# A two-stage spectral kernel: one row tile per PSUM bank in the second stage, and reloadable weight buffers filled first

## The chip, the cores and the metric

The kernel runs on one core of one Trainium2 chip. The metric is the device time of one execution in microseconds (us), the median of several runs. A ratio is the mean time of one kernel's fast runs over the mean time of the other kernel's fast runs of the same rounds, so it is not quite the ratio of the medians quoted beside it. A run counts as slow when it lies more than 1.5% above the fastest run of its kernel; the ratios leave slow runs out, the medians quoted do not.

## The reference

```
x: (8, 3264, 192)                     8 batches, 3264 positions, 192 channels
a  = causal 7-tap convolution of x, softmaxed taps per head (8 heads of 24 channels)
X  = rfft(a, axis=1)[:, :64]          64 modes
Y  = X @ (w_r + i w_i)[mode]          a 192x192 complex matrix for each mode
y  = irfft(Y, n=3264)
u  = a + y
out = u + relu(u @ w_ch)
```

The kernel never forms `u`. It keeps `a` in bf16 and uses `u @ w_ch = a @ w_ch + y @ w_ch`, with the 64 modes multiplied by `w_ch` beforehand ("weight products").

## The kernel before

It has three stages.

1. *First stage* (to 80 us): x is loaded by GpSimd's DMA queue, convolved by banded matmuls, and projected on 64 cosines and 64 sines.
2. *Mix stage* (80 to 111 us): sixteen groups of four modes. Each group needs 2 x 288 KB of weights. "Mix g" is 12 short matmuls. In between PE transposes `a` into `cc` (channels on the partitions) and the cosine and sine table, in "jobs" of one PSUM bank each; VectorE and ACT copy the banks out.
3. *Second stage* (from 111 us): 50 "duos" of two row blocks x two batches, one item for the row ends ("h"), and two items that compute further weight products. For each duo PE adds a channel part `a @ w_ch` and a table part (`g`, the modes already multiplied by `w_ch`), ACT applies relu, PE adds the table part `y`, VectorE adds `a` and writes an output buffer that SyncE stores.

The matmuls of the second stage contract over 64 partitions, so two of them are issued as a pair of row tiles, on partitions 0 to 63 and 64 to 127. In the profile before the two of a pair run side by side: pairs of 192 columns follow one another every 0.08 us and pairs of 384 columns every 0.16 us, and single matmuls of 384 columns over 128 partitions also every 0.16 us. Before the change an item's bank holds both batches of one block, and its sums need both halves of the partitions: channels 0 to 63 and cosines below, channels 64 to 127 and sines above. The kernel lets the two row tiles work on two banks and then swap, and at each swap PE waits ("turn"; in the profile before a weight load stands still for 0.29 us there). Here no two row tiles of the second stage work on one bank at the same time, so what that would do is not shown. The turns in the kernel:

```python
def both(duo, zt, first, which, begin=False, end=False):
    lists = (z_pieces(duo[first], 0, which), z_pieces(duo[1 - first], 1, which))
    old = held.get(id(zt))
    if old is not None and old[0] != first and not begin:
        turn(old[1])                  # PE waits for its own last matmuls on these banks
    for k in range(...):
        for row in range(2):
            ...
            nc.tensor.matmul(zt[:, first ^ row, cols], l, r, ...)
```

The weights of the mix stage have nine buffers. Four lie in the part of `cc` that is filled last ("late") and can be used once; five lie in an arena and are used again:

```python
wts = [... for a, n in ((late, NL), (arena, NW)) for i in range(n)]     # NL = 4, NW = 5
def wbuf(g): return wts[g] if g < NL else wts[NL + (g - NL) % NW]
def mix(g):
    ...                                # 12 matmuls
    if g >= NL:
        load_w(g + NW)                 # group 9 is issued after mix 4
```

Of the kernel before, what the change touches and what calls it, by code (L numbers as in the profile page):

```python
# [19 lines left out]
def kernel(  # L20
# [32 lines left out]
    def sb(name, shape, dtype, **kw):  # L53
# [5 lines left out]
    NW = 5  # L59
# [3 lines left out]
    CB = 2 * NF + 1 + NT  # L63
    cc = sb("cc", [NQ, CB, P], BF16)
    cm, ct = cc[:, :, 0:CB - NT, :], cc[:, :, CB - NT:CB, :]
    ftab = sb("ftab", [NT + 1, 2 * MODES], BF16)

# [4 lines left out]
    zw = mixa[:, 0:2 * B * D].rearrange("p (b t d) -> p b t d", b=B, t=2)  # L72
# [3 lines left out]
    wt2 = sb("wt2", [D], BF16)  # L76
# [5 lines left out]
    ymix = [sb(f"ymix{i}", [2, D], BF16) for i in range(2)]  # L82
# [3 lines left out]
           for a, n in ((late, NL), (arena, NW)) for i in range(n)]  # L86

    def wbuf(g):
        return wts[g] if g < NL else wts[NL + (g - NL) % NW]

    NO = 7
    OB = 2 * 2 * 2 * D
    outs = [arena[:, OB * i:OB * (i + 1)].bitcast(F32).rearrange("p (k d) -> p k d", k=2) for i in range(NO)]
    pos = [0]
# [23 lines left out]
    midx = temp(MODES, F32)  # L118

# [37 lines left out]
    hs = [xall[HALF:P, NT:NSLOT:NT, 0, :], xall[0:HALF, NT:NSLOT:NT, 1, :]]  # L157
# [12 lines left out]
    for a in hs:  # L170
        nc.vector.memset(a, 0.0)
# [47 lines left out]
    for i in range(2):  # L219
        src = bass.AP(tensor=x.tensor, offset=x.offset + (i * S + P * NF) * D,  # L220
                      ap=[[D, HALF], [2 * S * D, NQ], [1, D]])
        nc.gpsimd.dma_start(out=xall[HALF * i:HALF * i + HALF, NT:NSLOT:NT, i, :], in_=src)
# [11 lines left out]
    for q in range(NQ):  # L234
        nc.gpsimd.memset(ct[0:HALF, q, NF, HALF:P], 0.0)
        nc.gpsimd.memset(ct[HALF:P, q, NF, 0:HALF], 0.0)
# [4 lines left out]
    for i in range(2):  # L241
        nc.gpsimd.dma_start(out=wt2[64 * i:64 * i + 64, :], in_=moe_w_ch[P:D, :])
# [12 lines left out]
    def conv_step(q, t0, n, half, step):  # L255
# [8 lines left out]
        for j in range(2):  # L264
            for own in (True, False):
# [6 lines left out]
                if own:  # L272
                    ms = [(LO, LO, o, cur, 0), (UP, UP, o, cur, 0)]
                    if last:
                        ms.append((UP, UP, o[:, n - 1, 1, :], xall[:, s0 + n - 1, 1, dsl], 64))
                else:
                    ms = [(LO, UP, o, cur, 0), (UP, LO, o[:, k0:n, :, :], prev, 64)]
# [29 lines left out]
    def dft_unit(q, t0, n):  # L307
        xp = low[0][:, 0:2 * D]
        for t in range(t0, t0 + n):
            if t < NF:  # L310
                nc.tensor.matmul(xp, ftab[:, t, :], xall[:, slot(q, t), :, :], start=(t == 0), stop=False,  # L311
                                 skip_group_check=True)
            else:
                for i in range(2):
                    nc.tensor.matmul(xp[:, D * i:D * i + D], ftab[:, NF + i, :], xall[:, slot(q, t), i, :],
                                     start=False, stop=(i == 1), skip_group_check=True)
# [32 lines left out]
    def g_bank(t0, n):  # L349
        tp = next_bank()  # L350
        for k in range(n):
            nc.tensor.transpose(tp[:, P * k:P * k + P], ftab[:, t0 + k, :], ident[:])
        copy(ftab[:, t0:t0 + n, :].rearrange("p t s -> p (t s)"), tp[:, 0:P * n])

    def cm_bank(q, b0, n):
        tp = next_bank()
        nf = min(n, 2 * NF - b0)
        for k in range(nf + 2 * (n - nf)):
            t, i = divmod(b0 + k, 2)
            nc.tensor.transpose(tp[:, P * k:P * k + P], xall[:, slot(q, t), i, 0:P], ident[:])  # L360
        copy(cm[:, q, b0:b0 + nf, :].rearrange("p t s -> p (t s)"), tp[:, 0:P * nf])
        if nf < n:

            srcv = tp[:, P * nf:P * nf + 6 * HALF].rearrange("p (k s) -> p k s", k=2)[:, :, 0:HALF]
            nc.vector.tensor_copy(out=cm[:, q, 2 * NF, :].rearrange("p (k s) -> p k s", k=2), in_=srcv)

    def ct_bank(q, t0, n):
        tp = next_bank()
        for k in range(n):
            for i in range(2):  # L370
                nc.tensor.transpose(tp[64 * i:64 * i + 64, P * k:P * k + P], xall[:, slot(q, t0 + k), i, P:D],  # L371
                                    ident[:], tile_position=(0, 64 * i))
        nf = min(n, NF - t0)
        copy(ct[:, q, t0:t0 + nf, :].rearrange("p t s -> p (t s)"), tp[:, 0:P * nf])
        if nf < n:
            for i in range(2):
                r = slice(HALF * i, HALF * i + HALF)
                nc.vector.tensor_copy(out=ct[r, q, NF, r], in_=tp[r, P * nf + HALF * i:P * nf + HALF * i + HALF])
# [3 lines left out]
    nb = 2 * NF + 1  # L382
    for q in range(NQ):
        js = [((8 * k + 7) // 2, cm_bank, q, 8 * k, min(8, nb - 8 * k)) for k in range((nb + 7) // 8)]
        js += [(8 * k + 7, ct_bank, q, 8 * k, min(8, NT - 8 * k)) for k in range((NT + 7) // 8)]
        js.sort(key=lambda j: j[0])
        tjobs += [(NT * q + min(j[0], NF),) + j[1:] for j in js]
# [6 lines left out]

    waiting = []
    for k, u in enumerate(units):
# [5 lines left out]
        if k:  # L402
# [4 lines left out]
            if k > 1:  # L407
                some(1 + k % 2 if k < 14 else 1, min(NT * q + t0 + n, NT * (NQ - 1)))
# [14 lines left out]
    def mix(g):  # L423
# [7 lines left out]
        if g >= NL:  # L431
            load_w(g + NW)

    def mix_copy(d):
        nc.scalar.copy(out=ymix[d % 2][:], in_=low[d % 2][:, 0:2 * D].rearrange("p (g d) -> p g d", g=2))

    def mix_trans(d):
        ets = [low[2 + t][:, :].bitcast(BF16)[:, 0:2 * P].rearrange("p (g k) -> p g k", g=2) for t in range(2)]
        for t in range(2):
            for g in range(2):  # L440
                nc.tensor.transpose(ets[t][:, g, :], ymix[d % 2][:, g, 64 * t:64 * t + P], ident[:])
        for t in range(2):
            dst = yet[:, t, :, :].rearrange("p (c m) b -> p m c b", c=2)[:, 8 * d:8 * d + 8, :, :]
            srcv = ets[t].rearrange("p g (q k) -> p (g q) k", q=4)[:, :, 0:16].rearrange("p m (c b) -> p m c b", c=2)
# [10 lines left out]
    tjobs = [(0, g_bank, 8 * k, min(8, NTM - 8 * k)) for k in range((NTM + 7) // 8)] + tjobs  # L455
    some(2)


    def z_pieces(u, row, which):

        r = slice(64 * row, 64 * row + 64)
        res = []
        if u[0] == "h":
            for k, q in enumerate(u[1]):
                cols = slice(D * k, D * k + D)
                if which == "c":
                    res.append((cols, cm[r, q, 2 * NF, :], wm[r, 0:D]))
                    res.append((cols, ct[r, q, NF, :], wt2[r, :]))
                else:
                    for i in range(2):  # L470
                        res.append((cols, ftab[r, NF + i, :], zw[r, 2 * q + i, 0 if which == "g" else 1, :]))
        else:
            q, t = u
            if which == "c":
                for i in range(2):
                    res.append((slice(D * i, D * i + D), cm[r, q, 2 * t + i, :], wm[r, 0:D]))
                res.append((slice(D * row, D * row + D), ct[r, q, t, :], wt2[r, :]))
            else:
                res.append((slice(0, 2 * D), ftab[r, t, :],
                            zw[r, 2 * q:2 * q + 2, 0 if which == "g" else 1, :]))  # L480
        return res

    held = {}

    def both(duo, zt, first, which, begin=False, end=False):


        lists = (z_pieces(duo[first], 0, which), z_pieces(duo[1 - first], 1, which))
        old = held.get(id(zt))
        if old is not None and old[0] != first and not begin:  # L490
            turn(old[1])
        last = [None, None]
        for k in range(max(len(lists[0]), len(lists[1]))):
            for row in range(2):
                lst, bank = lists[row], first ^ row
                if k >= len(lst):
                    continue
                cols, l, r = lst[k]
                mm = nc.tensor.matmul(zt[:, bank, cols], l, r, start=(begin and k == 0),  # L499
                                      stop=(end and k == len(lst) - 1), skip_group_check=True)  # L500
                last[row] = mm.ins.name
        held[id(zt)] = (first, last)

    def zw_batch(b, zt, k):
        nc.tensor.matmul(zt[:, k, 0:2 * D], yet[:, 0, :, b], wm[:], start=True, stop=False)
        nc.tensor.matmul(zt[:, k, 0:2 * D], yet[:, 1, :, b], w1[:], start=False, stop=True)

    def zw_copy(b, n, src, act):
        dst = zw[:, b:b + n, :, :].rearrange("p b t d -> p b (t d)")
# [7 lines left out]
    for k, item in ((14, 2), (20, 3), (22, (("h", (0, 1)), ("h", (2, 3))))):  # L517
# [5 lines left out]
    def finish(n):  # L523
        duo, zt = items[n]
        o = outs[n % NO]
        if duo[0][0] == "h":
            for i in range(2):
                r = slice(HALF * i, HALF * i + HALF)
                nc.vector.tensor_tensor(out=o[r, :, :].rearrange("p k (a d) -> p k a d", a=2),  # L529
                                        in0=zt[r, :, 0:2 * D].rearrange("p k (a d) -> p k a d", a=2),  # L530
# [118 lines left out]
```

## Time and profile before

| kernel before (profiled run, span 189.7 us) | start, us |
|---|---|
| last mix | 111.36 |
| first output add on VectorE | 119.23 |
| last output add | 183.49 |
| end of the span | 189.7 |

The time is 191.55 us (the median of three runs, 190.38 to 191.63). These four points cut the run into pieces: what sets the last mix, the passage to the first add, the adds, the tail. The lines of the profile itself stand in the prediction.

### The profile page before, as it was taken

To read this page: it belongs to the slowest core of one execution; us is meant where nothing else is said; L and a number is where in the kernel's file an instruction comes from. 1 tells how busy PE (TensorE), PEld (TensorE's weight loads), DVE (VectorE), ACT (ScalarE), POOL (GpSimd) and SP (SyncE) were. 2 spreads that over 40 slices of the span, in tenths; PEclk is the share of its full clock that TensorE was granted. 3 is DMA by queue.
4 is the path that set the end of the run, shared out by engine and by line. 5 is a ranking of instruction groups with operands and counts; after the bars stand their busy time and mean duration, and the time that the engine had idled before them with its cause. 6 is when DMAs were issued, how large, how long until landed. Compare 5 with 4: busy or idle time off the path is not lost.

```text
span 189.7 us, 6202 instructions
## 1 busy us (share of the span) xinstructions
PE 154.9 (82%) x2687; PEld 102.3 (54%) x2687; DVE 116.5 (61%) x178; ACT 94.2 (50%) x129; POOL 66.6 (35%) x115
## 2 busy tenths in 40 slices
PE   0046579999999999898739749999999999999950
PEld 0023347766666756665427423666667566666620
DVE  4879555686677757464413302678575977777770
ACT  2066745545653553444523215566665666666630
POOL 7998899669557734105731000000000000000000
PEclk9999978999999999999985975999999999999997
DMA  5999999999999999995999920489986799999993
GB/s 55 147 188 189 190 173 178 191 191 192 189 190 178 178 203 207 206 207 81 199 196 205 206 46 0 152 271 363 304 274 223 225 362 323 328 325 324 327 327 133
DMA packets 63179, 40.07 MB, mean 211 GB/s; under 512 B 28848, under 2 KB 63152, under 8 KB 63152
## 3 DMA queue, kind: packets, MB, share of 16 engines
q0 software_dynamic: 36000, 19.59, 76.0%
q1 hardware_dynamic: 27152, 20.09, 31.7%
q8 instruction: 21, 0.34, 0.7%
q14 instruction: 6, 0.05, 0.1%
HBM read 39.20 MB, written 20.05 MB: 312 GB/s over the span
## 4 chain that ended last, share of the span: by engine, by line
PE 67%; DMA 13%; POOL 7%; issue 4%; DVE 4%; ACT 2%; POOLq 0%; DVEq 0%; ACTq 0%
PE zb L499 17%; PE za L499 16%; PE z L285 11%; PE low L311 9%; DMA arena<-in_moe_w_i_dram 6%; DMA arena<-in_moe_w_r_dram 4%; PE low L360 4%; POOL xall L140 4%; DMA xall<-in_x_dram 3%; PE low L371 3%; POOL arena L417 1%; PE low L324 1%; PE low L428 1%; DVE xall L305 1%; ACT za L521 1%
## 5 line engine op out<-in xcount | busy, mean ns | idle before, releaser
L285 PE MATMUL z<-xall,band 64*64 64x192 bf16 (+2 forms) x800 | 27.2, 265 | 17.5 <-DVE band L188 11.6
L140 POOL DMA_DIRECT2D xall<-in_x_dram x48 | 38.2, 810 | 7.0 <-DMA xall<-in_x_dram 5.0
L499 PEld LDWEIGHTS <-cc 64*128 64x128 bf16 x616 | 24.4, 94 | 21.2 <-PE za L499 7.3
L499 PE MATMUL za<-mixa,ftab 64*128 64x384 bf16 x208 | 32.7, 331 | 0.6 <-ACT za L521 0.3
L305 DVE CAST xall<-z 128x768 bf16<-128x768 f32 (+1 forms) x24 | 24.5, 1021 | 13.6 <-PE z L285 12.1
L540 DVE TENSOR_TENSOR arena<-za,xall 128x768 f32<-128x768 f32 x26 | 24.8, 956 | 10.8 <-PE za L499 4.5
L285 PEld LDWEIGHTS <-band 64*64 64x64 bf16 x800 | 18.1, 110 | 24.5 <-ACT band L186 12.0
L499 PE MATMUL zb<-mixa,ftab 64*128 64x384 bf16 (+1 forms) x224 | 31.2, 311 | 0.1
L303 ACT CAST xall<-z 128x768 bf16<-128x768 f32 (+1 forms) x24 | 20.4, 851 | 15.1 <-PE z L285 13.8
L540 DVE TENSOR_TENSOR arena<-zb,xall 128x768 f32<-128x768 f32 x24 | 22.9, 957 | 7.5 <-ACT za L521 4.0
L521 ACT ACTIVATE za<-za 128x768 f32<-128x768 f32 x26 | 20.7, 795 | 11.1 <-PE za L499 11.1
L521 ACT ACTIVATE zb<-zb 128x768 f32<-128x768 f32 x25 | 19.9, 795 | 12.3 <-PE zb L499 12.3
L499 PEld LDWEIGHTS <-ftab 64*128 64x128 bf16 x432 | 19.6, 94 | 4.2 <-issue 2.1
L311 PE MATMUL low<-xall,ftab 128*128 128x384 bf16 x100 | 21.6, 343 | 0.0
L499 PE MATMUL za<-wm,cc 64*128 64x192 bf16 x208 | 17.4, 245 | 0.2
L499 PE MATMUL zb<-wm,cc 64*128 64x192 bf16 x200 | 17.1, 248 | 0.4 <-DVE arena L529 0.3
L360 PEld LDWEIGHTS <-xall 128*128 128x128 bf16 x208 | 14.0, 103 | 3.2 <-issue 0.5
L340 DVE COPY cc<-low 128x1024 bf16<-128x1024 bf16 (+2 forms) x19 | 11.8, 620 | 4.4 <-PE low L360 2.3
L340 DVE COPY cc<-r 128x1024 bf16<-128x1024 bf16 (+2 forms) x10 | 6.0, 604 | 13.7 <-PE r L371 8.3
L338 ACT COPY cc<-low 128x1024 bf16<-128x1024 bf16 (+1 forms) x9 | 8.5, 941 | 11.4 <-PE low L371 5.1
L417 POOL DMA_DIRECT2D arena<-in_moe_w_r_dram x12 | 7.6, 632 | 17.1 <-PE low L428 10.4
L499 PE MATMUL za<-wt,cc 64*128 64x192 bf16 x104 | 12.8, 243 | 0.0
(104 smaller groups left out, 175.0 us busy)
## 6 DMA issues: line engine op xcount, KB each, us to landing
out_dram<-arena SPq DMA_DIRECT2D x46, 384.0 KB, 3.9
xall<-in_x_dram POOLq DMA_DIRECT2D x24, 192.0 KB, 8.1
xall<-in_x_dram POOLq DMA_DIRECT2D x16, 240.0 KB, 7.1
arena<-in_moe_w_r_dram POOLq DMA_DIRECT2D x12, 288.0 KB, 11.1
arena<-in_moe_w_i_dram POOLq DMA_DIRECT2D x12, 288.0 KB, 11.2
out_dram<-arena SPq DMA_DIRECT2D x10, 192.0 KB, 2.9
xall<-in_x_dram POOLq DMA_DIRECT2D x8, 144.0 KB, 7.0
cc<-in_moe_w_r_dram POOLq DMA_DIRECT2D x4, 288.0 KB, 7.2
```

Of the source, the lines that this page charges most:

```text
L140: nc.gpsimd.dma_start(out=xall[:, s0:s0 + nf, i, :], in_=src)
L285: mm = nc.tensor.matmul(ov[c], band[r, h, c.start + shift + 64 * (r is UP and c is LO): c.start + shift + 64 * (r is UP and c is LO) + 64] ...
L303: nc.scalar.copy(out=dst, in_=srcv)
L305: nc.vector.tensor_copy(out=dst, in_=srcv)
L311: nc.tensor.matmul(xp, ftab[:, t, :], xall[:, slot(q, t), :, :], start=(t == 0), stop=False, skip_group_check=True)
L338: nc.scalar.copy(out=out, in_=in_)
L340: nc.vector.tensor_copy(out=out, in_=in_)
L360: nc.tensor.transpose(tp[:, P * k:P * k + P], xall[:, slot(q, t), i, 0:P], ident[:])
L417: nc.gpsimd.dma_start(out=wbuf(g)[64 * half:64 * half + 64, :, :, :], in_=src[4 * g:4 * g + 4, :, :].rearrange("m (p j) e -> p m j e", j=3))
L499: mm = nc.tensor.matmul(zt[:, bank, cols], l, r, start=(begin and k == 0), stop=(end and k == len(lst) - 1), skip_group_check=True)
L521: nc.scalar.activation(out=zt[:, :, 0:2 * D], in_=zt[:, :, 0:2 * D], func=ACT.Relu)
L540: nc.vector.tensor_tensor(out=o[:, :, :], in0=zt[:, :, 0:2 * D], in1=xall[:, s[0]:s[1] + 1:s[1] - s[0], :, :].rearrange("p k i d -> p k (i ...
```

## The change

The intent is to let the row tiles run without turns. Each bank now belongs to one row tile: the even batch of a pair lies in the lower half of the partitions with all its 192 channels (three pieces of 64), the odd batch in the upper half. The tables must then stand in both halves: a cosine table and a sine table (`tabs`), each twice. The transposes become pairs of 64-column ones, the weight products are made per half, the row ends become one item of 128 rows, the last pair of mixes is copied out in two halves, the channel parts of the first two items move behind the last mix, the last item is stored in two parts, and the arena's buffers are filled before the late ones. Space for the second table comes from the arena: four buffers there instead of five, and six output buffers instead of seven.

```diff
-    NW = 5
+    NW = 4
-           for a, n in ((late, NL), (arena, NW)) for i in range(n)]
+           for a, n in ((arena, NW), (late, NL)) for i in range(n)]
-        if g >= NL:
+        if g < NW:
+            load_w(g + NW + NL)
+        elif g >= NW + NL:
             load_w(g + NW)
...
+    def twin_bank(src, dst, n):
+        tp = next_bank()
+        for k in range(n):
+            for i in range(2):
+                nc.tensor.transpose(tp[64 * i:64 * i + 64, P * k:P * k + P], src(k, i), ident[:],
+                                    tile_position=(0, 64 * i))
+        copy(dst.rearrange("p t s -> p (t s)"), tp[:, 0:P * n])
...
+    def c_part(n):
+        for k, (q, t) in enumerate(duo):
+            for j in range(3):
+                for i, r in enumerate(ROWS):
+                    nc.tensor.matmul(zt[:, i, D * k:D * k + D], cc[r, q, 3 * t + j, :], wc[r, j, :], ...)
+    def m_part(n, which):
+        for c in range(2):
+            for k, w, q, t in parts:
+                for i, r in enumerate(ROWS):
+                    nc.tensor.matmul(zt[:, i, D * k:D * (k + w)], tabs[c][r, t, :], zw[r, q:q + w, c, which, :], ...)
...
+    PLAN = (1, 2, 1, 2, 1, 2, 1, 2, 3, 3, 3, 3, 3, 3, 99)     # transpose jobs after each mix
+    XJOBS = [k % 3 != 1 for k in range(len(units))]           # jobs in the first stage: 15, before 28
...
     for n in range(N + 1):
+        m_part(n, 0); relu(items[n][1])
+        c_part(n + 1)
+        m_part(n - 1, 1); finish(n - 1)
```

## The prediction

> **What bounds the kernel now.** I first read the two busy strips and the traffic strips of the page (40 slices of 4.74 us), since a mean over the run mixes three stages.
>
> ```profile
> PE   0046579999999999898739749999999999999950
> PEclk9999978999999999999985975999999999999997
> DMA  5999999999999999995999920489986799999993
> GB/s 55 147 188 189 190 173 178 191 191 192 189 190 178 178 203 207 206 207 81 199 196 205 206 46 0 152 271 363 304 274 223 225 362 323 328 325 324 327 327 133
> ```
>
> Until about 111 us the DMA is full: x, then sixteen groups of mode weights, come in at 190 to 207 GB/s. There is one hole, slice 18 (81 GB/s). PE is full from 25 to 80 us, thins out to 3 to 7 tenths while it waits for weights, and is full again to the end while the output leaves at about 325 GB/s. The clock falls in slices 20, 22 and 24. So: loads set the end of the first part, and either PE or the stores set the second.
>
> Next, the stretches of one microsecond around the hole and around the start of the second stage (columns: stretch, length, busy time and count of PE, PEld, DVE, ACT, POOL; then granted clock, DMA share, GB/s).
>
> ```profile
> 85.00:86.00 1.00, 0.94 (x20) 0.62 (x20) 0.00 (x0) 0.97 (x2) 0.00 (x0) 1.00 1.20 203
> 86.00:87.00 1.00, 0.52 (x12) 0.42 (x16) 0.89 (x2) 0.51 (x3) 0.00 (x0) 1.00 0.62 105
> 87.00:88.00 1.00, 1.00 (x40) 0.78 (x32) 0.15 (x2) 0.18 (x1) 0.42 (x1) 1.00 0.09 15
> 88.00:89.00 1.00, 0.69 (x19) 0.39 (x11) 0.56 (x1) 0.67 (x2) 1.00 (x3) 1.00 0.28 27
> 89.00:90.00 1.00, 1.00 (x28) 0.67 (x30) 0.43 (x3) 0.35 (x2) 1.00 (x3) 1.00 0.76 90
> 115.00:116.00 1.00, 1.00 (x5) 0.27 (x3) 0.59 (x1) 0.35 (x2) 0.00 (x0) 0.50 0.00 0
> 119.00:120.00 1.00, 1.00 (x20) 0.80 (x20) 0.77 (x1) 0.29 (x1) 0.00 (x0) 1.00 0.00 0
> ```
>
> The four stretches from 86 us move 105 + 15 + 27 + 90 = 237 KB, where 205 GB/s would move 820: 2.84 us of loading are lost. The wait list and the timeline say why.
>
> ```profile
> POOL arena L417 <- PE low L428: 10.4, 1, 10.4
> 87.58 0.61 POOL L417 DMA_DIRECT2D arena<-in_moe_w_r_dram  x1 [10.37 <-PE low L428]
> 111.36 0.46 PE L428 MATMUL low<-arena,mixa 128*16 128x192 bf16 x12 [1.58 <-DMA arena<-in_moe_w_i_dram]
> ```
>
> GpSimd stood 10.4 us before it could issue group 9: that group's buffer is the arena's first, which group 4 used, and group 4 is mixed only at about 87 us. After that seven groups need 20.6 us, and the last mix starts at 111.36 us, on the landing of its weights. From there to the first output add (119.23 us, VectorE timeline) 7.87 us pass at a clock of 0.50 until about 118.6 us.
>
> Last, the steady second stage (start, length, engine).
>
> ```profile
> 128.81 0.20 PEld L499 LDWEIGHTS <-cc 64*128 64x128 bf16 x6 [0.29 <-PE zb L499]
> 128.81 0.34 PE L499 MATMUL zb<-wm,cc 64*128 64x192 bf16 x4
> 129.40 0.33 PE L499 MATMUL zb<-wm,cc 64*128 64x192 bf16 x4
> 130.04 0.34 PE L499 MATMUL zb<-wm,cc 64*128 64x192 bf16 x4
> 128.16 0.96 DVE L540 TENSOR_TENSOR arena<-zb,xall 128x768 f32<-128x768 f32 x1 [0.64 <-ACT za L521]
> 128.22 0.80 ACT L521 ACTIVATE za<-za 128x768 f32<-128x768 f32 x1 [0.43 <-PE za L499]
> ```
>
> Halves start at 128.81, 129.40 and 130.04: 0.59 + 0.64, a duo every 1.22 us. ACT needs 0.80 and VectorE 0.96 of it, so PE sets the pace. The weight load that stands still for 0.29 us is the "turn": before a bank passes from one row tile to the other, PE waits for the other's results. VectorE is nowhere held by a store, so the DMA is near its limit but not the bound.
>
> [...] in the trace a pair of 192 columns costs 0.08 us and a pair of 384 columns 0.163 us, one matmul's streaming time. [...]
>
> **The change, part by part.**
>
> *Turns.* Per duo both kernels stream 12 matmuls of 192 columns and 8 of 384, in pairs: 6 x 0.0815 + 4 x 0.163 = 1.14 us. The period is 1.22, so the two turns cost 0.08 us net. Over 51 items: 4.1 us. All of it is on the path, as PE is the bound here.
>
> *The item of row ends.* Two adds of 0.95 us on 64 partitions become one on 128. In the trace PE stands about 0.9 us for it near 148 us. As 64x64 tiles this item's matmuls cost 12 x 0.0815 + 8 x 0.163 = 2.28 us against 24 x 0.0815 = 1.96 before. Net gain 0.6 us.
>
> *Weight buffers.* Groups 0 to 4 now lie in the arena, 5 to 8 in the late region, so group 9 may be issued after mix 0. Mix 0 comes at 81.7 us now, and earlier after the change; the queue runs dry only at 86.4 us. The hole goes: -2.84 us. Against it the channel weights are loaded three times wider (2 x 72 KB for 2 x 24 KB): 98 KB at 200 GB/s = +0.5 us. The last weights then land near 111.36 - 2.84 + 0.5 = 109.0 us.
>
> *Transposes.* By the instruction order, the first stage goes from 136 full + 136 half transposes to 236 halves: from 17 x 0.45 + 8.5 x 0.57 = 12.5 us (chain rows of 8 and of 16) to 14.75 x 0.57 = 8.4 us. So the mix stage begins near 76 instead of 80 us; no gain by itself, since loads set its end. The mix stage takes 492 halves: 31 x 0.57 = 17.5 us; with 16 x 0.46 us of mixes and 8 x 0.4 us of transposes of their results that is 28 us of 33. PSUM copies are 48 in both. So it fits beneath the loads, and PE idles much less before the last mix.
>
> *From the last landing to the first add.* Before: 7.87 us, cold. If PE stays warm, the eight weight-product steps take 8 x 0.16 instead of 8 x 0.32 us (-1.3) and the first two duos run at full rate (-1.3); the channel parts of the first two items, formerly done in the wait, now come after the last mix, mostly beneath copies (+0.3): 5.5 us. If it goes cold anyway: about 8.4 us. I give warm 6 in 10: from 80.7 to 93 us the trace has nothing but transposes and mixes, PE about 85% busy, at clock 1.00.
>
> *Tail.* From the start of the last add (183.49 us) to the end 6.2 us; the last item's add and store are split over two queues, -0.5 us.
>
> Sum: first add at 109.0 + 5.5 = 114.5 (cold 117.4). The adds span 183.49 - 119.23 = 64.3 us now, less 4.1 and 0.6: 59.6. Last add at 174.1 (177.0), end of span 179.8 (182.7). The times stand 1.85 us above the span (191.55 - 189.7): 181.7 warm, 184.6 cold, weighted 182.9. I add 0.6 us for stores that hold the adds now and then: 183.5 us, 4.2% faster.
>
> **Rivals.**
>
> *Stores become the bound.* 384 KB per 1.14 us is 345 GB/s against 325 now, and there are six output buffers instead of seven. For: the DMA share is already 0.97[...]. Against: stretches of two to four microseconds run at 355 to 372 GB/s, and six buffers give 6.8 us while a store takes 0.96 us to write and 3.9 us to land. If stores stayed at 325 to 334 GB/s, the period would be 1.18 to 1.21 us and 2 to 4 us of the turns' gain would go: 186 to 187 us.
>
> *The mix stage becomes PE bound.* In the cold state 16 half transposes take 1.06 us (seen at 100.3 us); three such jobs, a mix of 0.7 and half of 0.6 make 4.2 us per group against 2.95 us of loading. Six groups so: +7 us, and the kernel would end at 190. Against: a PE this busy should warm up, as the trace does at 105 us after 5 us of continuous work.
>
> *Add and relu become the wait.* The bank of an item is wanted four items later. By the new order two opening table parts, one closing one and one channel part lie between: estimated from the pair times, 0.163 + 3 x 0.326 + 0.49 = 1.64 us from its last matmul's issue. The add's round trip is an estimate too: 0.38 (that matmul's 0.33 and a handover) + 0.96 + 0.1 = 1.44 us. Only 0.2 us to spare; if VectorE slows by that over its new four-dimensional pattern, the turns' gain is lost: 186 to 187 us.
>
> **Range and chances.** The three gains are independent in kind (loads 2.3, turns and row ends 4.7, clock up to 2.6, tail 0.5). Losing half of them still leaves 186. Range 179.5 to 187.5; faster by over 2% (below 187.7) 0.87, within 2% 0.11, slower 0.02.
>
> **What would show it.** Right: no dip below 190 GB/s between 60 us and the last load; GpSimd's 10.4 us wait before group 9 gone; the last mix at 108 to 110 us; clock 1.00 when the relus begin; a duo every 1.14 to 1.16 us and no weight load held by PE's own results; VectorE at 0.96 us. Wrong: adds held by stores, a period still near 1.2, PE without idle time and at clock 0.5 between 90 and 109 us, or a last mix later than 111 us.

## The result, and the profile after

The changed kernel takes 184.32 us (183.6 to 184.46) against 190.97 us in the same rounds: a ratio of 0.965, with an interval of 0.959 to 0.972. It was timed twice more in later rounds (e5, and e10, which turned out to be the same program): 0.971 and 0.969. So it is 3 to 3.5% faster. Predicted were 183.5 us, with a range of 179.5 to 187.5.

First the same strips of the page, of the changed kernel (40 slices of 4.57 us).

```profile
PE   0047889999798979869997679999999999999930
PEclk9999999999999999999999999999999999999995
DMA  4999999999999999999999940399987699999993
GB/s 50 159 184 189 190 191 189 191 190 188 191 191 173 187 197 206 206 207 183 206 207 205 207 85 4 106 339 319 335 297 250 188 361 367 359 341 346 347 357 115
```

The hole of 81 GB/s has become a dip to 183 in slice 18 (slices are counted from 0; the prediction's sign, no dip below 190, was missed by this little), and the loads end in slice 23: in the trace their last packet ends at 107.84 us, and the last landing is reported at 108.16 us. The clock strip has no dip left before the last slice. The stores run at up to 367 GB/s.

Next the timeline of the mix stage: the first reload, transposes before which PE stood still ("issue"), and the last mix.

```profile
81.47 0.61 POOL L403 DMA_DIRECT2D arena<-in_moe_w_r_dram  x1 [6.78 <-PE low L414]
...
97.52 1.14 PE L356 MATMUL r<-ident,xall 128*64 128x128 bf16 x34 [1.31 <-issue]
...
103.44 0.92 PE L356 MATMUL r<-ident,xall 128*64 128x128 bf16 x26 [1.59 <-issue]
...
106.85 0.92 PE L356 MATMUL r<-ident,xall 128*64 128x128 bf16 x26
108.81 0.69 PE L356 MATMUL r<-ident,xall 128*64 128x128 bf16 x18 [1.04 <-issue]
109.44 0.29 PE L430 MATMUL low<-ident,xs 128*128 128x128 bf16 x2
109.65 0.46 PE L414 MATMUL low<-arena,mixa 128*16 128x192 bf16 x12
```

GpSimd issues the first reload at 81.5 us, 6.1 us earlier than before. But the last mix has no wait for its weights any more (no "<-DMA" behind it, where before it had 1.58 us). PE arrives late instead, 1.5 us after the last landing: three times, and last in the middle of a transpose job (1.04 us), it stood still, and the profile shows nothing that it waited for ("issue").

Last, the adds of VectorE: before, then after. The first rows are the start of the second stage, the last row the last item.

```profile
119.23 0.96 DVE L540 TENSOR_TENSOR arena<-za,xall 128x768 f32<-128x768 f32 x1 [3.20 <-PE za L499]
120.45 0.96 DVE L540 TENSOR_TENSOR arena<-za,xall 128x768 f32<-128x768 f32 x1 [0.26 <-PE za L499]
...
183.49 0.96 DVE L540 TENSOR_TENSOR arena<-za,xall 128x768 f32<-128x768 f32 x1
```

```profile
115.37 0.96 DVE L536 TENSOR_TENSOR arena<-za,xall 128x768 f32<-128x768 f32 x1 [1.59 <-PE za L485]
116.53 0.96 DVE L536 TENSOR_TENSOR arena<-za,xall 128x768 f32<-128x768 f32 x1 [0.20 <-ACT zb L508]
...
171.89 0.96 DVE L536 TENSOR_TENSOR arena<-za,xall 128x768 f32<-128x768 f32 x1 [0.19 <-ACT za L508]
173.03 0.96 DVE L536 TENSOR_TENSOR arena<-za,xall 128x768 f32<-128x768 f32 x1 [0.18 <-ACT zb L508]
...
175.92 1.01 DVE L529 TENSOR_TENSOR arena<-za,xall 128x384 f32<-128x384 f32 x2
```

The adds are as long as before (0.96 us) and now follow one another every 1.14 to 1.16 us instead of 1.22; in between VectorE waits 0.2 us for its inputs and never for a store. From such lines comes the account of the gain:

| piece, us | before | after | difference | predicted (warm case) |
|---|---|---|---|---|
| start to last mix | 111.36 | 109.65 | -1.71 | -2.34 |
| last mix to first add | 7.87 | 5.72 | -2.15 | -2.37 |
| first add to last add | 64.26 | 60.55 | -3.71 | -4.7 |
| last add to end | 6.2 | 6.8 | +0.6 | -0.5 |
| span | 189.7 | 182.7 | -7.0 | -9.9 |

The last row is the warm case alone; the forecast then allowed for a cold clock and for stores.

### The profile page after: what moved, and what is told of

Read it like the earlier page. It is cut to its first block, busy times and chain, and to the rows that moved or that the text cites.

```text
span 182.7 us, 6843 instructions
## 1 busy us (share of the span) xinstructions
PE 151.0 (83%) x3012; PEld 107.9 (59%) x3012; DVE 113.6 (62%) x166; ACT 95.7 (52%) x131; POOL 65.6 (36%) x107
## 3 DMA queue, kind: packets, MB, share of 16 engines
q0 software_dynamic: 36256, 19.69, 79.0%
HBM read 39.40 MB, written 20.05 MB: 325 GB/s over the span
## 4 chain that ended last, share of the span: by engine, by line
PE 77%; DVE 6%; issue 6%; ACT 6%; POOL 1%; DVEq 0%; POOLq 0%; ACTq 0%
PE z L287 13%; PE za L485 10%; PE r L356 9%; PE low L313 9%; PE zb L485 8%; PE za L466 7%; PE zb L466 7%; PE low L356 5%; PE low L414 3%; DVE arena L183 2%; PE low L430 1%; ACT xall L305 1%; PE low L326 1%; POOL xall L145 1%; ACT cc L340 1%
## 5 line engine op out<-in xcount | busy, mean ns | idle before, releaser
L287 PE MATMUL z<-xall,band 64*64 64x192 bf16 (+3 forms) x800 | 28.7, 271 | 17.2 <-ACT band L189 10.9
L356 PEld LDWEIGHTS <-xall 128*64 128x64 bf16 x624 | 19.2, 112 | 10.9 <-issue 9.7
L485 PE MATMUL za<-mixa,ftab 64*128 64x384 bf16 (+1 forms) x112 | 17.3, 312 | 0.6 <-ACT za L508 0.6
L466 PE MATMUL za<-wc,cc 64*128 64x192 bf16 x312 | 17.3, 243 | 0.3 <-ACT cc L340 0.3
L485 PE MATMUL za<-mixa,fsin 64*128 64x384 bf16 (+1 forms) x112 | 17.2, 311 | 0.0
L356 PE MATMUL r<-ident,xall 128*64 128x128 bf16 x388 | 13.5, 220 | 4.2 <-issue 4.2
L342 DVE COPY cc<-r 128x1024 bf16<-128x1024 bf16 (+1 forms) x16 | 10.3, 672 | 10.6 <-PE r L356 7.0
L466 PE MATMUL zb<-wc,cc 64*128 64x192 bf16 x288 | 15.9, 243 | 0.0
L485 PE MATMUL zb<-mixa,ftab 64*128 64x384 bf16 (+1 forms) x104 | 15.9, 310 | 0.0
L485 PE MATMUL zb<-mixa,fsin 64*128 64x384 bf16 (+1 forms) x104 | 15.9, 310 | 0.0
```

Of the source, the lines that this page charges most:

```text
L287: mm = nc.tensor.matmul(ov[c], band[r, h, c.start + shift + 64 * (r is UP and c is LO): c.start + shift + 64 * (r is UP and c is LO) + 64] ...
L342: nc.vector.tensor_copy(out=out, in_=in_)
L356: nc.tensor.transpose(tp[64 * i:64 * i + 64, P * k:P * k + P], src(k, i), ident[:], tile_position=(0, 64 * i))
L466: nc.tensor.matmul(zt[:, i, D * k:D * k + D], cc[r, q, 3 * t + j, :], wc[r, j, :], start=(k == 0 and j == 0), stop=False, skip_group_check ...
L485: nc.tensor.matmul(zt[:, i, D * k:D * (k + w)], tabs[c][r, t, :], zw[r, q:q + w, c, which, :], start=False, stop=end and k + w == 2, skip_ ...
```

## The experiments

Twelve runs were made, of ten new kernels (e5 and, as it turned out, e10 are the changed kernel again). All profiles are of fast runs; single slow runs among the timed ones (one each in e3, e4 and e10, and two of the kernel before, in the rounds of e9 to e12) are left out of the ratios. Eleven gave a result within the tolerance or were wrong as stated; one did not do what it was meant to (e10).

**e1: the buffer order undone in the changed kernel.**

```diff
-           for a, n in ((arena, NW), (late, NL)) for i in range(n)]
+           for a, n in ((late, NL), (arena, NW)) for i in range(n)]
```

(with the matching index and the reload after mix 4 again)

> The changed kernel with one part undone: the late buffers first, the reloadable ones second, so the first reload (group 8) is issued after mix 4 instead of mix 0. Theory (loads set the end of the first part): the load queue runs dry at about 83 us and refills at about 88 us, the last mix comes 3 to 4 us later (112.5 to 113.5 instead of 109.65 us), the time rises from 184.3 to about 187.5 us. Rival (the first part is bound by PE with its transposes and instruction fetches, loads have slack): last mix within 1 us of 109.65, time within 1 us of 184.3.

Measured: 187.6 us, ratio 0.978 against 0.965 to 0.971 of the changed kernel. The timeline:

```profile
112.88 0.46 PE L414 MATMUL low<-arena,mixa 128*16 128x192 bf16 x12 [0.87 <-DMA arena<-in_moe_w_i_dram]
```

The last mix is 3.2 us later and waits for its weights again; the traffic strip has one slice at 14 GB/s. By the ratios the order of the buffers is worth 1.3 to 2.4 us of time in the changed kernel, by the position of the last mix 3.2.

**e2: the buffer order alone, in the kernel before** (the mirror image of that edit).

> The kernel before with only the buffer order of the change. Theory: the hole at 86 to 90 us closes, the last mix moves from 111.36 to about 108.5 us, PE is still cold (clock 0.5) at the start of the second stage, period still 1.22 us, time 2.8 us less than before (about 188.2 for 191). Rival (the hole was slack): time as before.

Measured: 188.64 us, ratio 0.984, so 3.1 us of 191. The timeline:

```profile
108.58 0.47 PE L428 MATMUL low<-arena,mixa 128*16 128x192 bf16 x12 [1.57 <-DMA arena<-in_moe_w_i_dram]
```

The last mix comes 2.78 us earlier, on its weights; the loading that the hole lost had been worked out as 2.84. The period of the adds stays at 1.22 to 1.23. In this profile the clock was at half from 110.1 to 113.5 us only, so the passage to the first add took 7.27 us. The theory is confirmed; almost half of the change's gain can be had by these few lines.

**e3: one wait put back per item in the changed kernel.**

```diff
+            if which == 0 and c == 0:
+                past = recent[-2:]       # the last pair issued before this item's
+            if which == 0 and c == 1 and past:
+                turn(past)
```

> The changed kernel with one wait put back per item: before the second pair of an item's opening table matmuls PE waits for the last pair issued before the first. No data needs it. Theory (PE's own issue sets the pace of the second stage, so that a wait of PE on its results goes one to one into the time): period 1.145 us rises by the wait, estimated 0.06 to 0.10 us, to about 1.22; time +3 to +5 us (187.5 to 189). Rival (adds or stores set the pace): period and time unchanged within 1 us.

Measured: 186.87 us, ratio 0.974. The wait shows as 0.29 us in which a weight load stands, exactly as before the change, and the adds are back at the old pace:

```profile
115.59 0.96 DVE L543 TENSOR_TENSOR arena<-za,xall 128x768 f32<-128x768 f32 x1 [1.59 <-PE za L491]
116.82 0.96 DVE L543 TENSOR_TENSOR arena<-za,xall 128x768 f32<-128x768 f32 x1 [0.27 <-ACT zb L515]
118.06 0.96 DVE L543 TENSOR_TENSOR arena<-zb,xall 128x768 f32<-128x768 f32 x1 [0.29 <-ACT zb L515]
```

From the first to the last add it takes 179.41 - 115.59 = 63.8 us instead of 60.55. So PE sets the pace, and the wait goes into the adds: of the 0.29 us for which the weight load stands, 0.08 us is left in each period, +3.3 us over all adds. The time grew by less than the 3 to 5 us expected: 0.974 against 0.965 to 0.971 is 0.5 to 1.6 us. The tail was 0.7 us shorter here (6.1 instead of 6.8 us); the rest lies within the spread of the timed runs and stays open.

**e4: the clock.** Transpose jobs are moved earlier, so that PE has little to do before the last mix.

```diff
-    PLAN = (1, 2, 1, 2, 1, 2, 1, 2, 3, 3, 3, 3, 3, 3, 99)
+    PLAN = (1, 2, 1, 2, 1, 2, 1, 2, 5, 5, 5, 4, 2, 0, 99)
```

> The changed kernel with its transposes moved earlier in the mix stage, so that PE stands almost idle from about 102 us to the last mix, as before the change. Theory (the warm clock is worth 2 to 3 us): clock 0.5 from the last mix on, first add about 8 us after the last mix instead of 5.7; the last mix itself comes up to 1.6 us earlier because no transpose or instruction fetch stands before it; time between -0.5 and +1.5 us of 184.3. Rival (the hops over ACT and VectorE set this stretch, the clock is no matter): first add 5.7 us after the last mix, time about 1.5 us less.

Measured: 185.91 us, ratio 0.967. The clock was at half from 110.0 to 113.4 us. The last mix came at 110.26 us, not earlier: mixes 10 and 11 were delayed by the jobs (98.42 and 101.06 us instead of 95.23 and 98.58), so the last reloads were issued later, and the last mix waited 0.52 us for their landing. The first add followed 6.66 us after it, where the changed kernel takes 5.72. So 3.4 us of cold clock cost 0.94 us of this passage, not the 2.3 us expected. In the kernel before the cold stretch was twice as long, 111.8 to 118.6 us. The theory holds in kind; the timed runs cannot tell the kernels apart.

**e5: the changed kernel again**, as the measure for e6 to e8.

> The changed kernel as it is, as the measure for the others of this call: 184.3 us, 0.965 of before, last mix at 109.65 us, first add 5.7 us later, period 1.145 us, 6.8 us from the start of the last add to the end.

Measured: 185.28 us, ratio 0.971. In its profile the last mix comes at 110.67 us, since the first stage was 1.0 us later (mix 0 at 81.74 us; it had a cold stretch at 25 us, and its mean granted clock was 0.977 against 0.986); the passage (5.74 us), the period and the tail (6.8 us) are as before. This is the run-to-run spread: about 1 us at the start of the second stage.

**e6: half of the stores**.

```diff
-                          ap=[[D, P], [S * D, 4], [1, D]])
-            nc.sync.dma_start(out=dst, in_=ov)
+                          ap=[[D, P], [S * D, 2], [1, D]])
+            nc.sync.dma_start(out=dst, in_=ov[:, 0:2, :])
...
-            for i in range(2):
+            for i in range(1):
```

> Wrong on purpose: every store but those of the row ends and of the last item carries only half of its rows (the output is incomplete). Theory (PE sets the period, and the stores only lengthen the tail by queueing behind one another): period still 1.145 us, the end comes about 2 to 3 us after the last add instead of 5.8, time 1 to 2 us less than the changed kernel. Rival (stores hold the second stage): period falls below 1.1 us, time at least 4 us less.

Measured: 181.96 us, ratio 0.953. The adds take 176.08 - 115.24 = 60.8 us as with all stores, so stores do not hold the second stage. But the end comes 180.2 - 176.08 = 4.1 us after the start of the last add instead of 6.8 (3.1 us after its end, where 2 to 3 were expected). The time fell by 3.5 us against e5, more than expected; about 1 us of that is the start of the second stage, which differs by as much between these two profiles. What SyncE waits for at the end (first the changed kernel, then e6; total, number, longest):

```profile
SPq L632 <- DMA out_dram<-arena: 4.2, 1, 4.2
```

```profile
SPq L632 <- DMA out_dram<-arena: 1.7, 3, 0.7
```

With full stores SyncE waits 4.2 us for the last landing; with half of them three waits make 1.7 us in all. At about 350 GB/s a queue builds up by the end, and it is paid for after the last add.

**e7: no transposes between the last two mixes.**

```diff
+    PLAN = (1, 2, 1, 2, 1, 2, 1, 2, 4, 3, 4, 3, 4, 3, 99)
```

> The changed kernel with the last three transpose jobs moved from behind mix 14 to behind mixes 8, 10 and 12, so that only the half copy and its transposes stand between mix 14 and mix 15. Theory (the last mix waits for PE, which stands about 1 us for its next instructions in the middle of those jobs, and not for its weights, which land by 107.8 us): last mix at 108.0 to 108.5 instead of 109.65 us and still warm, time 1.0 to 1.6 us less. Rival (the weights land last): last mix unchanged; or PE goes cold for 3.4 us and loses 0.9 us of it again.

Measured: 186.52 us, ratio 0.981; the last mix at 110.55 us. A miss. The timeline says why:

```profile
105.84 1.36 PE L356 MATMUL r<-ident,xall 128*64 128x128 bf16 x42
108.81 0.25 PE L356 MATMUL r<-ident,xall 128*64 128x128 bf16 x2 [1.61 <-issue]
```

The stop has not gone with the jobs; it stands before other transposes and ends at the same 108.81 us. After it come mix 14 (109.31 us) and a wait of 0.56 us for ACT's copy of its result, which the jobs had covered before. Counting PE's records in the trace (matmuls, weight loads and 32 of its sequencer) shows a pattern: in the changed kernel PE stops before records 3265, 3521 and 3777, in e7 before 3265, 3521 and 3777 again, though other work stands there. These numbers are 256 apart. The stops of the first stage (0.96, 0.77, 1.03 and 0.53 us before records 1217, 1473, 1985 and 2241) lie on the same grid. The program's instructions come through a DMA queue of their own (page, queues: packets, MB, share), before and after:

```profile
q8 instruction: 21, 0.34, 0.7%
```

```profile
q8 instruction: 23, 0.38, 0.8%
```

In the trace each of the 23 packets has 16384 bytes. PE has 6056 records in all, and 6056 / 256 = 23.7 (before 5406 / 256 = 21.1 with 21 packets). From these counts one packet is estimated to be a block of 256 instructions of PE. The times of the packets agree with a PE that stands until its next packet is there. In the changed kernel the packets of the three blocks end at 96.11, 102.14 and 107.33 us, and PE goes on 1.41, 1.30 and 1.48 us after each. They had begun 3.0 to 3.7 us after PE started on the 256 records before. In the second stage, beside stores at up to 367 GB/s, they begin at most 1.5 us after it, and no stop is left on the grid there.

The change brought more and shorter PE instructions into a stretch in which the loads run at 205 to 206 GB/s: PE now goes through 256 records in 5.4 to 5.9 us there (stop included), where the kernel before took 9.7 and 11.1 us (records 2753 to 3265). The profiled run of e7 was one of its best: its runs with a mean clock of 0.994 and 0.984 took 185.0 and 185.3 us, the four at 0.957 to 0.969 took 186.3 to 187.6. Those four have no trace, so where their clock fell was not shown.

**e8: e7, with the second item's channel part after the weight products.**

```diff
     mix_trans(NG // 2 - 1, slice(1, 2))
-    c_part(1)
     for k, z in enumerate((low[0], low[2], low[3], low[1])):
         ...
+    c_part(1)
```

> As e7, and the channel part of the second item issued after the weight products instead of before them, where PE waits for copies anyway. Theory: first add 5.4 instead of 5.7 us after the last mix, time about 0.3 us below e7, so some 1.5 us below the changed kernel (182.7). Rival: the copies of the products end this stretch, nothing gained over e7.

Measured: 186.27 us, ratio 0.976, not faster. The clock went to half from 109.7 to 113.1 us in its profile, and the first add came 6.8 us after the last mix, where e7, with the same jobs but warm, took 5.37. Whether the new order is worth anything when warm stays open.

**e9: more jobs in the first stage.**

```diff
-    XJOBS = [k % 3 != 1 for k in range(len(units))]
+    XJOBS = [1 for k in range(len(units))]
```

(and two jobs a group from group 8 on)

> The changed kernel with 22 instead of 15 transpose jobs in the first stage and 26 instead of 33 in the mix stage (two a group from group 8 on). Theory (in the changed kernel PE, with its transposes and its waits for instructions, and not the loads, sets the last mix; the first stage has room for jobs, since it ended at 79.2 us with 15 as it had at 79.7 with 28): first stage ends within 1.5 us of 79.2, last mix on its weights at 107.8 to 108.8 us instead of 109.65 to 110.67, time 1 to 1.5 us less than the changed kernel if PE stays warm, about the same if it goes cold. Rival (loads set the last mix): no gain.

Measured: 188.67 us, ratio 0.990: slower by some 4 us. The first stage had no room. It ended near 86.2 us (part of that is a cold stretch from 49.0 to 55.8 us and a stop of 2.5 us before record 1217 in the profiled run), mix 0 came at 87.67 us, after the load queue had run dry, and the loads had a full slice at zero:

```profile
GB/s 54 155 188 189 190 191 189 191 191 190 191 190 170 192 204 207 205 149 0 147 207 205 206 208 51 3 317 294 365 283 317 142 334 369 354 346 351 324 371 134
```

The last mix (115.11 us) then waited for its weights again. So the stages are tied: the first reload needs mix 0, and mix 0 needs the end of the first stage.

**e10: shifting the instruction blocks** with 210 empty PE instructions at the start.

> The changed kernel with 210 empty PE instructions before its first matmul, where PE stands idle until 24 us anyway. Theory (PE's stops of 1.0 to 1.6 us in the mix stage come every 256 instructions of its stream[...], whatever work stands there): the stops move 210 matmul or weight-load records earlier (from records 3265, 3521, 3777 to about 3055, 3311, 3567), the next one falls at or after the last mix when the loads are done, the last mix comes 0.5 to 1.5 us earlier, time 0 to 1.5 us less. Rival (the stops belong to the work that stands there, e.g. PSUM banks coming free): they stay at records 3265, 3521, 3777 and nothing moves.

Measured: 184.62 us, ratio 0.969. The experiment failed: the empty instructions did not reach the program, whose profile counts 6843 instructions like that of the changed kernel, and the grid has not moved. It is a third measurement of that kernel. Two things can be read from it. Its long stops in the mix stage stood before records 3009 and 3265 (1.07 and 1.85 us; 0.35 us before 3521). The places are fixed by the grid; at which of them PE stops varies, and so does the last mix (108.95 us here). And its clock was at half from 98.5 to 101.9 us, in the middle of the mix stage: this program does not stay warm there in every run.

**e11: half of the reloads**, wrong on purpose in its weights (the small contribution of the modes left the result within the tolerance).

```diff
             for half, src in ((0, moe_w_r), (1, moe_w_i)):
+                if half and g >= NW + NL:
+                    continue
```

> Wrong on purpose: the changed kernel without the second load of each group from 8 on (the imaginary weights stay those of an earlier group), so the loads end near 95 us. Theory (in the changed kernel PE sets the last mix, by its work and by stops for instructions that come late only while the load queues are full): no stop of over 0.5 us after the loads end, last mix at 106 to 108 us instead of 109 to 110.7, time 2 to 3 us less. Rival A (the weights' landing sets the last mix): it moves to 100 us or earlier. Rival B (the stops have nothing to do with the loads): stops at records 3521 and 3777 as before and the last mix unchanged.

Measured: 180.51 us, ratio 0.948. The loads ended at 102.8 us (last landing at 103.1), later than the 95 us expected. The last mix:

```profile
106.23 0.46 PE L416 MATMUL low<-arena,mixa 128*16 128x192 bf16 x12
```

It came 2.7 to 4.4 us earlier than in the three profiles of the changed kernel and that of e12 below (108.95 to 110.67 us). The one stop over 0.5 us that remained in the mix stage, 0.62 us before record 3521 at 101.25 us, fell before the loads ended. The last mix did not follow the weights to 103.1 us (rival A), and the stops did not stay as they were (rival B). So in the changed kernel PE sets the last mix: its own work ends at about 106 us, and stops for instructions, 3.3 to 4.2 us in these profiles, carry it past the landing of the weights. But not far past it: in the same four profiles (e12 included) the last mix starts 0.9 to 1.5 us after the last landing (108.02 to 109.78 us). Without the stops the loads would hold it again, so by this estimate the stops of the mix stage cost the kernel 0.9 to 1.5 us, not 4; the rest of e11's gain comes from loads that ended earlier.

**e12: the last item added and stored whole** (the split switched off).

> The changed kernel with the last item added and stored whole, as before the change. My prediction's term: the split saves 0.5 us, so this should be 0.5 us slower. Rival (the last stores queue behind the others' backlog, so when the last one starts hardly matters): within 0.2 us of the changed kernel.

Measured: 183.94 us, ratio 0.965; from the start of the last add to the end 183.1 - 176.28 = 6.8 us, as with the split. The split saves nothing: what ends last is the queue of stores.

No version with a complete result and all its loads beat the changed kernel clearly; e12 is its equal with less code.

## Why the prediction was right, point by point

**The number: close, in part by luck.** The run was warm, and for the warm case the sum was 181.7 us, 2.8 us below the profiled run (184.46). The forecast of 183.5 had 1.2 us weighted in for a cold clock and 0.6 us for stores that hold the adds. Neither happened in the profiled run; what the warm sum had too low was the tail (1.1 us), the adds (1.0 us) and the last mix (0.6 us).

**Turns: right.** 4.1 us were predicted. 50 intervals that shorten from 1.22 to 1.145 us make 3.75 us; the adds shortened by 3.71, and e3, which puts a wait back, gives 3.3 of it back. PE was the bound of the second stage, as read from ACT's 0.80 and VectorE's 0.96 us.

**Row ends: the term was mis-sized.** 0.6 us were predicted. The adds exceed 50 regular periods by 64.26 - 61.0 = 3.3 us before and by 60.55 - 57.25 = 3.3 us after. Whatever the single add saved, the other irregular steps took. From the add before the second weight-product item to the second add after the row ends it took 7.11 us before and 6.98 after, where the faster pace alone would have brought 0.3 us; in it, the step across the weight products grew from 2.70 to 2.99 us. Why was not tested.

**Weight buffers: right, from a wrong count.** The prediction put five groups in the arena and spoke of group 9 after the change. The diff makes the arena four buffers, and it is group 8. The queue runs dry earlier by a group, at about 83 us, but mix 0 at 80.7 still comes before that. The value was right: 2.84 us worked out, 2.78 measured alone in e2.

**"So the mix stage begins near 76": wrong.** Mix 0 came at 80.70 us, 1.0 us earlier than before (81.68), though some 4 us of transposes had left the first stage. The stops on the grid of 256 records make 3.7 us there in the changed kernel and 0.5 us in the kernel before. By its size this accounts for the missing 3 us; no run separates it. It is what the step below left out, met earlier.

**"So it fits beneath the loads": this is the step that failed.** The last weights landed at 108.16 us, earlier even than the 109.0 predicted, and PE was late by itself, at 109.65. The sum of PE's work was right in order of size: 28 us were predicted for the mix stage, and e11 took 25.4 from the start of mix 0 to the end of the last mix. What it left out were the stops for instructions, 1.31, 1.59 and 1.04 us in the profile of the changed kernel. Without them PE would have been ready at about 105.7 us (an estimate: 109.65 less their sum), and the landing would have set the last mix as predicted. The second rival, a mix stage bound by PE, came true by a way that it did not name: the clock stayed at full speed (in this profile; not in e10's), the instruction supply did not.

**Clock: right in kind.** The passage shortened by 2.15 us where 2.37 were predicted for the warm case. e4 shows 0.94 us for a cold stretch half as long as in the kernel before, e8 against e7 1.4 us (with another order of the passage); in the old order, with half of the cold stretch gone, e2's passage was 0.6 us shorter. How much of the 2.15 us is the clock and how much the new order of the passage is not separated.

**Tail: wrong by 1.1 us.** Predicted -0.5, measured +0.6. e12 shows that the split has no effect, and e6 that stores make 2.7 us of the tail. This is the store rival, true only at the end: the adds never waited for a store. The 0.6 us itself lies within the spread: with all stores, tails from 6.1 to 6.8 us occurred, and e2, with the old pace, had 186.8 - 180.07 = 6.7.

**Add and relu as the wait: did not happen.** VectorE's add kept its 0.96 us with the new access pattern and waited 0.2 us per item.

**A misreading that cost nothing.** The clock strip before dips in slices 5, 6, 20, 21, 23 and 24, not in 20, 22 and 24. No term of the sum rests on it.

## What to carry to other kernels

When two row tiles share banks by turns, look for a layout in which each bank belongs to one tile; the price is a table stored twice, and the gain can be read off beforehand as the period minus the sum of the streaming times (here 1.22 - 1.14 us). Fill the buffers that can be reloaded first, and the ones that can't last. Work that "fits" under full load queues should be counted in instructions as well as in microseconds: here PE stood still for 1.31, 1.59 and 1.04 us before three records 256 apart while the loads ran at 206 GB/s, and at none of these places in the second stage, where the stores moved up to 367 GB/s.

## What the traces show of the hardware beside this

- Beside loads at 206 GB/s PE's stops on the grid of 256 records were up to 1.9 us long in the mix stages of these runs, three of them 3.9 us in one mix stage; with half of the loads one of over 0.5 us was left, 0.62 us. In the second stage of the changed kernel there was none.
- In the changed kernel PE did little but transposes and short mixes from 80.7 to 109.6 us, and the granted clock stayed at 1.00 throughout; in e10 it had fallen to half and rose again at 101.9 us, after 3.4 us of the same mixture. The mixes, 12 short matmuls each, are part of it, and the traces do not separate what the transposes alone would do. In the kernel before the clock fell at 111.79 us; from 107.6 us until then PE had been busy for 2.1 of 4.2 us.
- The weights landed at 206 GB/s in bf16 and were read in float32, twice as many bytes (39.40 MB read for 19.69 MB landed over the whole run): about 412 GB/s by this estimate, for 18 us. The stores reached 372 GB/s over two microseconds in the kernel before.
- In the changed kernel the packet of the next 256 instructions (by the estimate under e7) began at most 1.5 us after PE started on the 256 records before in the second stage, but 3.0 to 3.7 us after it at the three stops beside the loads; PE went on 1.3 to 1.5 us after the packet's end.
